# Chunk 1's row tiles 8 to 15 as seven half-size products, half of w1's block sums on GpSimd, and the ninth chunk's attention in two blocks

## The chip, the cores and the metric

The kernel runs on one core of a Trainium2 chip. The engines of the core are named here as the profile names them: PE (TensorE, matrix products; PEld is its loading of weights), DVE (VectorE), ACT (ScalarE), POOL (GpSimd) and SP (SyncE, which here only starts transfers). The metric is the device time of one execution in microseconds. The kernel before takes 268.32 us, the median of three runs (268.29 to 269.69).

## What is computed

Linear attention over 8 batches, 8 heads, 576 positions and 64 features per head, and behind it a layer norm with a two-layer MLP and a residual:

```python
q_s = exp(q) / sum(exp(q), axis=-1)          # the max that is subtracted cancels
k_s = exp(k) / sum(exp(k), axis=2)           # over the positions
kv  = einsum('bhsd,bhse->bhde', k_s, v)
x   = einsum('bhsd,bhde->bhse', q_s, kv)     # then (b, s, 512)
xn  = (x - mean) / sqrt(var + 1e-6) * g_ln
out = x + relu(xn @ w_ch1) @ w_ch2           # 512 -> 2048 -> 512
```

## The kernel before

**Chunks.** The rows are cut into nine chunks of 512. Chunk c (0 to 7) holds positions 0 to 511 of batch c, as four tiles (t) of 128 rows. The ninth chunk, `C9` = 8, gathers the last 64 positions of all eight batches. The MLP works on the transposed, centred rows `xnT`; w1 with the gain folded in is `w1g`; the scale of the norm (`rstd`) is applied only at the output (`y_quarter`).

**First MLP stage.** It makes the hidden values `hT` (2048 rows in 16 row tiles m of 128, times 512 columns). Chunks 2 to 8 use `mm1_fast`: Strassen's scheme in Winograd's form on 2 by 2 blocks, with seven half-size products in place of eight. A group g is four row tiles (m = 4g to 4g+3); each product of a group is four matmuls of 256 columns (`prod1`). The products need sums and differences of blocks of `w1g` (`w1_q`, made by `sum_w1`, in two parts: part 0 serves groups 0 and 1, part 1 groups 2 and 3) and of blocks of `xnT` (`tq`, made by `sum_x`). Their results are copied and added in PSUM by ACT (`seed`, `copy_5`, the relus) and DVE (`add_5`, `out_22`). Chunk 0 uses plain products throughout (`mm1_part`). Chunk 1 is mixed: row tiles 0 to 7 by `mm1_part` with 256 columns, row tiles 8 to 15 by `mm1` with 512 columns, 32 matmuls.

**Second MLP stage.** `mm2_fast` is the same scheme for chunks 1 to 8. `sum_h` (DVE) makes its sums `hs` from `hT`, `quarter_w2` (DVE) those of w2 (`w2_q`).

**Order.** All engines work through lists written by hand: `run(main, side)` issues PE's main steps in order, counts their weights (one 512-column matmul is 1, one of 256 columns 0.5) and lets each entry of the side list, a pair of position and function, go out when the count has reached its position. Every engine executes its own instructions in the order in which they were issued. While chunk c goes through the MLP, the side list carries the attention of chunk c+1 and the loads and exponentials of chunk c+2. For chunk 1 that list is `second_side`; for chunk 7 it is `attn_rest`, the attention of the ninth chunk. Chunk 1 has 120 units of weight.

**What the attention steps do.** `exp_q` and `exp_k` (ACT), `eq_T` (a transposing transfer), `reduce_q` and `recip_q` (DVE), `kv_pairs` (40 small PE matmuls, then DVE's normalisation into `kv_sb`), `po_mm` (four PE matmuls per tile into the PSUM tile `po`, of which there are two), `x_fast` (DVE: reads `po`, frees it, and writes x and the centred `xn`), `xn_T` (a transposing transfer into `xnT`), `square_sum` and `rstd_op` (ACT). In the ninth chunk `po_mm` issues eight matmuls of 64 output columns per tile.

**Buffers that matter here.** One SBUF buffer, tag `tq`, holds in turn the raw v of a batch (`vt`, loaded by `load_v` on POOL's queue for batches 1 to 3 and copied out by `cast_v` on DVE) and the sums `tq` of `sum_x`. So a load of v waits for the last reader of the sums before it, and the sums wait for `cast_v`. `load_batch(3, (2,), ...)` loads q of batch 3; a tiny POOL copy from `eqT` lets it go, and SP issues the transfer. PSUM has six banks for the MLP.

Of the kernel before, what the change touches and what calls it, by code (L numbers as in the profile page):

```python
# [12 lines left out]
FP32 = mybir.dt.float32  # L13
BF16 = mybir.dt.bfloat16
AF = mybir.ActivationFunctionType
# [5 lines left out]
def kernel(  # L21
# [16 lines left out]
    nc = tc.nc  # L38
# [5 lines left out]
    T = 4  # L44
# [177 lines left out]
    def sum_w1(i, part):  # L222
# [10 lines left out]
        )[i]  # L233
        for ko in range(2):
            nc.vector.tensor_tensor(out=dst[:, ko], in0=x[:, ko], in1=y[:, ko], op=op)
# [230 lines left out]
    def relu(i, dst, src, fast):  # L466
        if i % 8 == 7 and not fast:
            nc.vector.tensor_scalar_max(dst, in0=src, scalar1=0.0)
        else:
            nc.scalar.activation(dst, src, AF.Relu)  # L470

# [4 lines left out]

    def mm1(c, m, ko):
        if m == 0 and ko == 0:
            new_h()
        if ko == 0:  # L480
            hbox["ph"] = mm_ps.tile([P, T, P], FP32, tag="m", name="ph")
        nc.tensor.matmul(
            hbox["ph"], w1g[:, ko, m * P : (m + 1) * P], xnTs[c][:, :, ko, :],
            start=(ko == 0), stop=(ko == KO1 - 1),
        )
        if ko == KO1 - 1:
            relu(m, hbox["h"][:, m], hbox["ph"], c >= FAST)

    def mm1_part(c, m, t0, tn, ko):
# [4 lines left out]
        if m % 2 == 0 and at == 0 and ko == 0:  # L494
# [5 lines left out]
            start=(ko == 0), stop=(ko == KO1 - 1),  # L500
        )
        if m % 2 == 1 and at + tn == 2 and ko == KO1 - 1:
            dst = hbox["h"][:, m - 1 : m + 1, 2 * half : 2 * half + 2]
            if c == 0 and half and (m // 2) % 2 == 1:
                nc.vector.tensor_scalar_max(dst, in0=ph, scalar1=0.0)
            else:
                nc.scalar.activation(dst, ph, AF.Relu)
# [19 lines left out]

    def mm2(c, t, ko):
        if ko == 0:
            hbox["pc"] = mm_ps.tile([P, DM], FP32, tag="m", name="pc")  # L530
        nc.tensor.matmul(
            hbox["pc"], hbox["h"][:, ko, t, :], w2_sb[:, ko, :],
            start=(ko == 0), stop=(ko == KO2 - 1),
        )
        if ko == KO2 - 1:
            y_out(c, t, hbox["pc"])
# [200 lines left out]
    def mm1_fast(c):  # L737
# [46 lines left out]
        steps.append((0, new_h))  # L784
        for g0 in (0, 2):
# [5 lines left out]
    def mlp_steps(c):  # L791
        if c > FAST:
            return mm1_fast(c) + mm2_fast(c)
        full = range(KO2)
        first, parts = [], ()
        if c == 0:
            full = range(0)
            parts = ((0, 0, 1), (0, 1, 1), (1, 0, 2), (2, 0, 2), (0, 2, 2), (1, 2, 2), (2, 2, 2), (3, 0, 2), (3, 2, 2))
        else:
            full, parts = range(8, KO2), ((0, 0, 2), (1, 0, 2), (0, 2, 2), (1, 2, 2))  # L800
# [5 lines left out]
        first += [(1, lambda m=m, ko=ko: mm1(c, m, ko)) for m in full for ko in range(KO1)]  # L806
# [5 lines left out]
        if c >= FAST:  # L812
            return first + mm2_fast(c)
        return first + [(1, lambda t=t, ko=ko: mm2(c, t, ko)) for t in range(T) for ko in range(KO2)]
# [49 lines left out]
    def second_side():  # L864

        s = [(p, lambda i=i: quarter_w2(i, 1)) for i, p in enumerate((8.5, 13, 44, 46))]
        s += [(8.0, lambda: xn_pT(1, 3, nc.vector))]
        s += [(3, lambda: exp_q(2, 0, 4)), (7, lambda: exp_q(2, 2, 4)), (7.2, lambda: eq_T(2))]
        s += [(42, lambda: square_sum(1, 2)), (67, lambda: square_sum(1, 3)), (71, lambda: rstd_op(1))]
        s += [(7.3, lambda: load_batch(3, (2,), eqTs[2][0:1, T - 1, NP - 1, 0:4])), (31, lambda: load_batch(3, (0,)))]  # L870
        s += [(9 + 2 * j, lambda j=j: cast_v(2, j)) for j in range(2)]
        s += [(7.4, lambda: load_v(3))]
        s += [(93 + j, lambda j=j: cast_v(3, j)) for j in range(2)]
# [3 lines left out]
        s += [(41, lambda: kv_pairs(2))]  # L877
        s += [(46, lambda: start_x(2))]
        for t, (p0, p1) in enumerate(((52, 54), (57, 59), (62, 65), (70, 74))):
            s += spread([lambda t=t, i=i: po_mm(2, t, i) for i in range(NP)], p0, p1)  # L880
            s += [(p1, lambda t=t: x_fast(2, t)), ((73, 82, 88, 94)[t], lambda t=t: square_sum(2, t))]
# [288 lines left out]
```

## Time and profile before

| | |
|---|---|
| median of 3 runs | 268.32 us |
| profiled execution, its own time | 267.75 us |
| its span in the trace | 266.0 us |
| PE busy | 259.9 us, 98% |
| DVE busy | 216.9 us, 82% |
| ACT busy | 177.9 us, 67% |
| POOL busy | 88.4 us, 33% |
| granted TensorE clock | 1.00 throughout |

The profiled execution took 1.75 us more than its span, and the median of the runs lies 0.57 us above the profiled one. Matmuls overlap in PE's pipeline, so the mean duration of one (273 ns for 256 columns) is longer than the distance between two of them; costs on PE are read from the distance. In a timeline line the columns are start, time from the first start to the last end, engine, line of the kernel, operation, output and inputs, shape and count, and in brackets the idle time before it with what ended it.

### The profile page before, as it was taken

The numbers are of one execution on the slowest core, as the hardware profiler recorded it, in microseconds if no ns is written. First come the engines' busy times: TensorE is split into PE (matmuls) and PEld (weight loads), VectorE is DVE, ScalarE is ACT, GpSimd is POOL, SyncE is SP. The second block draws the span as 40 slices with busy tenths as digits, with TensorE's granted clock in tenths as the row PEclk, the third lists the DMA queues.
The fourth block names the chain that finished last, engine by engine and source line by source line (L and its number), as shares of the span: only waits on it lengthen the run. The fifth ranks groups of instructions, "written<-read, shape, count | busy, mean of one in ns | idle before, by whom it ended". The sixth has DMA issues, their size and how long they took to land.

```text
span 266.0 us, 6662 instructions
## 1 busy us (share of the span) xinstructions
PE 259.9 (98%) x2624; PEld 220.1 (83%) x2627; DVE 216.9 (82%) x470; ACT 177.9 (67%) x345; POOL 88.4 (33%) x139
## 2 busy tenths in 40 slices
PE   8999999999999999999999999999999999999993
PEld 6788855675888898899889988998899888888882
DVE  4675895887999899789978997899789969877872
ACT  4557872697976886788678867886788378438400
POOL 3932226212059202940295049305500810030000
PEclk9999999999999999999999999999999999999999
DMA  6999999979975997799679957995813530422014
GB/s 191 249 207 206 330 220 298 267 184 254 192 142 145 330 160 111 229 288 93 136 246 277 128 95 239 296 144 108 240 40 73 105 142 7 76 81 79 2 39 118
DMA packets 82297, 45.00 MB, mean 169 GB/s; under 512 B 58005, under 2 KB 79001, under 8 KB 82266
## 3 DMA queue, kind: packets, MB, share of 16 engines
q0 software_dynamic: 32512, 22.29, 45.2%
q1 hardware_dynamic: 49162, 21.77, 37.3%
q10 hardware_dynamic: 592, 0.52, 0.6%
q8 instruction: 20, 0.33, 0.5%
q14 instruction: 11, 0.09, 0.1%
HBM read 36.70 MB, written 9.44 MB: 173 GB/s over the span
## 4 chain that ended last, share of the span: by engine, by line
PE 68%; DVE 0%; issue 0%
PE bx L734 18%; PE ba L589 18%; PE bb L734 9%; PE bb L589 5%; PE bc L734 5%; PE bc L589 5%; PE be L589 5%; PE po L360 2%; PE pkv L330 1%; PE po L367 1%; PE bd L589 0%; DVE yl L629 0%; DVE kt L1061 0%; DVE zq L211 0%
## 5 line engine op out<-in xcount | busy, mean ns | idle before, releaser
L589 PEld LDWEIGHTS <-hs 128*128 128x128 bf16 x512 | 49.5, 98 | 5.7
L734 PEld LDWEIGHTS <-w_q 128*128 128x128 bf16 x448 | 43.0, 98 | 5.5 <-issue 0.3
L249 POOL TENSOR_TENSOR tq<-xnT 128x256 bf16<-128x256 bf16 x24 | 15.9, 679 | 76.9 <-DMA xnT<-xn 62.6
L589 PEld LDWEIGHTS <-hT 128*128 128x128 bf16 x384 | 37.2, 98 | 4.4
L734 PEld LDWEIGHTS <-w1g 128*128 128x128 bf16 x336 | 32.2, 98 | 3.9
L589 PE MATMUL ba<-w_q,hs 128*128 128x256 bf16 x256 | 31.7, 273 | 0.0
L734 PE MATMUL bx<-tq,w_q 128*128 128x256 bf16 x224 | 29.0, 273 | 0.0
L765 DVE TENSOR_TENSOR bb<-bx,s 128x512 f32<-128x512 f32 x28 | 18.2, 695 | 12.3 <-ACT s L762 8.7
L758 ACT COPY bc<-bx 128x512 f32<-128x512 f32 x28 | 15.1, 585 | 16.8 <-PE bx L734 16.8
L411 DVE SCALAR_TENSOR_TENSOR x<-po,rq 128x512 bf16<-128x512 f32 x34 | 23.3, 686 | 2.3 <-PE po L360 2.1
L385 ACT ACTIVATE scrap<-x,mv 128x512 bf16<-128x512 bf16 x32 | 23.0, 719 | 1.6 <-DVE x L411 1.3
L606 POOL DMA_DIRECT2D out_dram<-ot x28 | 15.5, 558 | 23.4 <-DVE ot L600 23.4
L211 DVE TENSOR_REDUCE zq<-eq 128x16 f32<-128x1024 bf16 (+1 forms) x20 | 20.7, 1051 | 2.6 <-ACT eq L202 2.0
L573 DVE TENSOR_TENSOR hs<-hT 128x1024 bf16<-128x1024 bf16 x32 | 21.7, 686 | 0.6 <-ACT hT L776 0.5
L360 PE MATMUL po<-kv_sb,eqT 128*128 128x128 bf16 x128 | 21.2, 219 | 0.0
L768 DVE TENSOR_TENSOR hT<-bx,s 128x512 bf16<-128x512 f32 x28 | 18.0, 685 | 3.8 <-PE bx L734 3.8
L776 ACT ACTIVATE hT<-bc 128x512 bf16<-128x512 f32 x28 | 15.3, 594 | 8.4 <-PE bc L734 8.4
L776 ACT ACTIVATE hT<-bb 128x512 bf16<-128x512 f32 x28 | 15.2, 595 | 8.5 <-PE bb L734 8.5
L776 ACT ACTIVATE hT<-bx 128x512 bf16<-128x512 f32 x28 | 15.2, 598 | 3.3 <-PE bx L734 3.3
L614 ACT COPY s<-ba 128x512 f32<-128x512 f32 x15 | 8.7, 579 | 12.5 <-PE ba L589 7.8
L589 PE MATMUL ba<-w_sb,hT 128*128 128x256 bf16 x128 | 16.7, 273 | 0.0
L589 PE MATMUL bb<-w_q,hs 128*128 128x256 bf16 x128 | 16.6, 273 | 0.0
(148 smaller groups left out, 556.0 us busy)
## 6 DMA issues: line engine op xcount, KB each, us to landing
out_dram<-ot POOLq DMA_DIRECT2D x32, 256.0 KB, 6.3
qt<-in_q_dram SPq DMA_DIRECT2D x5, 1024.0 KB, 5.8
kt<-in_k_dram SPq DMA_DIRECT2D x5, 1024.0 KB, 12.6
w_raw<-in_moe_w_ch_dram POOLq DMA_DIRECT2D x4, 512.0 KB, 12.0
w_sb<-in_moe_w_ch_dram POOLq DMA_DIRECT2D x4, 512.0 KB, 17.4
qt<-in_q_dram POOLq DMA_DIRECT2D x2, 1024.0 KB, 15.6
kt<-in_k_dram POOLq DMA_DIRECT2D x2, 1024.0 KB, 15.4
vm<-in_v_dram POOLq DMA_DIRECT2D x16, 128.0 KB, 10.7
```

The source lines that it names most:

```text
L211: nc.vector.reduce_sum(eqs[c][1][:, ts], eqs[c][0][:, ts], axis=AX.X)
L249: eng.tensor_tensor(out=dst[:, t], in0=x[:, t], in1=y[:, t], op=ALU.subtract)
L360: nc.tensor.matmul(pobox["p"][:, i * P : i * P + P], eqTs[c][:, t, i, :], kv_sb[:, c, i, :], start=True, stop=True,)
L385: nc.scalar.activation(scrap, x[:, t], AF.Square, bias=mv[:, t, 0:1], scale=-float(DM), accum_out=mv[:, t, 1:2],)
L411: nc.vector.scalar_tensor_tensor(x[:, t].rearrange("p (h d) -> p h d", h=H), in0=pobox[c, t].rearrange("p (h d) -> p h d", h=H), scalar=1. ...
L573: nc.vector.tensor_tensor(out=dst, in0=x, in1=y, op=op)
L589: nc.tensor.matmul(hbox[bank][:, t], lhsT, rhs, start=first and (own or t == 0) and k == 0, stop=k == KH - 1, skip_group_check=True)
L606: nc.gpsimd.dma_start(out[c, 0:SM, :].rearrange("(p t) n -> p t n", t=T)[:, t], ybox[c, t])
L734: nc.tensor.matmul(dst[:, q], lhsT, rhs, start=first and q == 0 and ko == 0, stop=ko == 1, skip_group_check=True)
L765: nc.vector.tensor_tensor(out=at[g, "b"], in0=at[g, "x"], in1=at[g, "s"], op=ALU.add)
L768: nc.vector.tensor_tensor(out=h_out(g, 1, 1), in0=at[g, "x"], in1=at[g, "s"], op=ALU.add)
L776: nc.scalar.activation(h_out(g, odd, half), at[g, name], AF.Relu)
```

## The change

Three things.

First, row tiles 8 to 15 of chunk 1 go through `mm1_fast(1, (2,))`, groups 2 and 3. This takes 56 matmuls of 256 columns for 32 of 512, so that chunk 1 has 116 units of weight. It needs the x sums of chunk 1 (`sum_x(1, i)`, new, on POOL at position 9) and part 1 of the w1 sums, which is now made in chunk 0 on DVE, where part 0 was. Two of the eight relus of `mm1_part` in chunk 1 move from ACT to DVE.

Second, part 0 of the w1 sums, first needed in chunk 2, is made in chunk 1 on POOL (positions 40, 46, 62, 66). In the kernel before, part 1 was made in chunk 1 on DVE (30, 47, 58, 64). For room, chunk 1's other steps move: `cast_v(2)` ahead of the new sums, `load_v(3)` from 7.4 to 60.4 (behind the last reader of chunk 1's sums), q's load from 7.3 to 10, the last two `quarter_w2` from 44 and 46 to 33.9 and 37, `kv_pairs(2)` from 41 to 34, `po_mm` and `x_fast` forward by 5 to 11 units, most later steps by 4.

Third, in `attn_rest` the ninth chunk's `po_mm` goes out in two blocks of two tiles (14 and 58) instead of four blocks of one (14, 44, 58, 67).

The diff, without the removal of functions that nothing calls any more:

```diff
     def sum_w1(i, part):
...
+        eng = nc.vector if part else nc.gpsimd
         for ko in range(2):
-            nc.vector.tensor_tensor(out=dst[:, ko], in0=x[:, ko], in1=y[:, ko], op=op)
+            eng.tensor_tensor(out=dst[:, ko], in0=x[:, ko], in1=y[:, ko], op=op)
...
     def mm1_part(c, m, t0, tn, ko):
...
-            start=(ko == 0), stop=(ko == KO1 - 1),
+            start=(ko == 0 and at == 0 and m % 2 == 0), stop=(ko == KO1 - 1),
+            skip_group_check=True,
...
-            if c == 0 and half and (m // 2) % 2 == 1:
+            if half and (m // 2) % 2 == 1:
                 nc.vector.tensor_scalar_max(dst, in0=ph, scalar1=0.0)
...
-    def mm1_fast(c):
+    def mm1_fast(c, firsts=(0, 2)):
...
-        for g0 in (0, 2):
+        for g0 in firsts:
...
     def mlp_steps(c):
...
-        first += [(1, lambda m=m, ko=ko: mm1(c, m, ko)) for m in full for ko in range(KO1)]
...
-        if c >= FAST:
-            return first + mm2_fast(c)
+        return first + mm1_fast(c, (2,)) + mm2_fast(c)
...
     def second_side():
-        s = [(p, lambda i=i: quarter_w2(i, 1)) for i, p in enumerate((8.5, 13, 44, 46))]
+        s = [(p, lambda i=i: quarter_w2(i, 1)) for i, p in enumerate((9, 13, 33.9, 37))]
...
-        s += [(42, lambda: square_sum(1, 2)), (67, lambda: square_sum(1, 3)), (71, lambda: rstd_op(1))]
-        s += [(7.3, lambda: load_batch(3, (2,), eqTs[2][0:1, T - 1, NP - 1, 0:4])), (31, lambda: load_batch(3, (0,)))]
-        s += [(9 + 2 * j, lambda j=j: cast_v(2, j)) for j in range(2)]
-        s += [(7.4, lambda: load_v(3))]
-        s += [(93 + j, lambda j=j: cast_v(3, j)) for j in range(2)]
+        s += [(40, lambda: square_sum(1, 2)), (63, lambda: square_sum(1, 3)), (67, lambda: rstd_op(1))]
+        s += [(10, lambda: load_batch(3, (2,), eqTs[2][0:1, T - 1, NP - 1, 0:4])), (31, lambda: load_batch(3, (0,)))]
+        s += [(8.1 + j / 8, lambda j=j: cast_v(2, j)) for j in range(2)]
+        s += [(9.1 + i / 8, lambda i=i: sum_x(1, i)) for i in range(4)]
+        s += [(60.4, lambda: load_v(3))]
+        s += [(89 + j, lambda j=j: cast_v(3, j)) for j in range(2)]
...
-        s += [(41, lambda: kv_pairs(2))]
-        s += [(46, lambda: start_x(2))]
-        for t, (p0, p1) in enumerate(((52, 54), (57, 59), (62, 65), (70, 74))):
+        s += [(34, lambda: kv_pairs(2))]
+        s += [(40, lambda: start_x(2))]
+        for t, (p0, p1) in enumerate(((40.5, 45), (47, 52.6), (55, 60.5), (65, 69))):
...
-        s += [(p, lambda i=i: sum_w1(i, 1)) for i, p in enumerate((30, 47, 58, 64))]
+        s += [(p, lambda i=i: sum_w1(i, 0)) for i, p in enumerate((40, 46, 62, 66))]
...
     def attn_rest():
-        for t, (p0, p1, p2) in enumerate(((14, 22, 46), (44, 54, 62), (58, 66, 69), (67, 75, 77))):
+        for t, (p0, p1, p2) in enumerate(((14, 22, 46), (14, 54, 62), (58, 66, 69), (58, 75, 77))):
...
-            + [(p, lambda i=i: sum_w1(i, 0)) for i, p in enumerate((80, 84, 88, 92))]
+            + [(p, lambda i=i: sum_w1(i, 1)) for i, p in enumerate((80, 84, 88, 92))]
...
-            sums = [(57, 0)] if c == FAST else [(p, i) for i, p in enumerate((30, 41) if c == B - 1 else (30, 33, 41))]
+            sums = [(53, 0)] if c == FAST else [(p, i) for i, p in enumerate((30, 41) if c == B - 1 else (30, 33, 41))]
```

## The prediction

> **What bounds the kernel now.** I read the page first, then the chain of waits, then the timelines of PE, DVE and POOL around chunk 1 (51 to 81 us) and around the ninth chunk's attention (205 to 238 us), and last the transfers of chunk 1.
>
> ```profile
> PE 259.9 (98%) x2624; PEld 220.1 (83%) x2627; DVE 216.9 (82%) x470; ACT 177.9 (67%) x345; POOL 88.4 (33%) x139
> PE 68%; DVE 0%; issue 0%
> ```
>
> The last chain is PE alone: from 80.96 us to 261.6 us every step follows the one before it on PE. A matmul that goes away there is time won, unless another engine was just behind. So the distance between matmuls comes first, in PE's timeline:
>
> ```profile
> 61.16 2.55 PE L482 MATMUL ph<-xnT,w1g 128*128 128x512 bf16 x11
> 63.54 0.22 PE L360 MATMUL po<-kv_sb,eqT 128*128 128x128 bf16 x1
> 80.95 0.60 PE L734 MATMUL bb<-tq,w_q 128*128 128x256 bf16 x4 [0.17 <-DVE kt L1061]
> 82.26 1.04 PE L734 MATMUL bc<-xnT,w1g 128*128 128x256 bf16 x8
> 83.13 1.04 PE L734 MATMUL bx<-tq,w_q 128*128 128x256 bf16 x8
> ...
> 213.34 0.60 PE L734 MATMUL bc<-xnT,w1g 128*128 128x256 bf16 x4
> 213.87 0.41 PE L367 MATMUL po<-kv_sb,eqT 128*64 128x128 bf16 x8
> 214.22 0.61 PE L734 MATMUL bc<-xnT,w1g 128*128 128x256 bf16 x4
> ```
>
> Eleven 512-column matmuls from 61.16 to 63.54: 0.216 us each. Eight 256-column ones from 82.26 to 83.13: 0.109 us each. The line at 80.95 is PE's only wait after 23 us, 0.17 us. What it waited for is a PSUM bank: `bb` of the second group takes the bank that chunk 1's last `y_quarter` frees, and that DVE step ends there:
>
> ```profile
> 61.30 0.18 DVE L336 RECIPROCAL rzk<-pkv 128x4 f32<-128x4 f32 x1 [2.49 <-PE pkv L330]
> 75.28 0.76 DVE L135 COPY vm<-vt 128x1024 bf16<-128x1024 bf16 x2
> 80.03 0.87 DVE L600 SCALAR_TENSOR_TENSOR ot<-ba,rstd,x 128x256 f32<-128x256 f32 x2
> ...
> 61.30:81.00 19.70, 19.53 (x164) 15.15 (x163) 19.41 (x47) 15.18 (x33) 5.40 (x9) 1.00 1.00 193
> ```
>
> The last line is a stretch of windows: its length, then busy time of PE, PEld, DVE, ACT, POOL. DVE is busy 19.41 of 19.70 us (in chunk 2, 81 to 105.9 us, 23.02 of 24.90). In chunk 1 DVE is as full as PE and ends 0.17 us behind it, so what the change does to DVE there counts one for one.
>
> **PE's terms.** (a) 56 matmuls at 0.109 us (6.10) take the place of 32 at 0.216 (6.91): -0.81 us. `kv_pairs` and `po_mm` are the same instructions elsewhere in the stage, at no cost. (b) Without the block at 213.87 the next product would have started at 213.34 + 4 x 0.109 = 213.78; it started at 214.22, so a block costs 0.44 us. Its eight starts lie within 0.41 - 0.22 = 0.19 us, thus some 0.22 us is the eight matmuls and 0.22 us the turn to 64 columns and back. Four blocks become two of twice the matmuls: -0.44 us. The fourth tile's matmuls now need the PSUM tile that `x_fast` of the second tile frees. DVE ran that step at 223.53 and freed the tile at 224.21; PE reaches the fourth tile at about 224.38 (third block, 0.22 us earlier, then eight matmuls). It hides with 0.2 us to spare; if not, PE loses those tenths. PE is the chain from there to the end, so (b) stands whole.
>
> **DVE's ledger for chunk 1**, from the copy at 53.32 to the last `y_quarter` at 80.83 us: 27.5 us, of which it was idle 2.49, so 25.0 of work. Removed: four w1 sums, two adds each, 4 x 0.68 = 2.7. Added: two `add_5` and two `out_22` (0.61 each, by the distance of the pairs at L765 and L768), one max 0.34, two relus at 0.60 from PSUM (the row of L505 has 0.69 for one, overlapping): 4.0. Work after: 26.3, so DVE could end at 79.6 if it never stood. PE would be at the bank in question at 80.78 - 0.81 = 79.97. Thus with no DVE wait PE's 0.81 and the old wait of 0.17 are won, -0.98 us, with 0.37 us of slack; with waits of W on DVE beyond that slack, chunk 1 costs 79.6 + W - 80.95 = W - 1.35 us.
>
> ACT loses eight relus and two more that go to DVE, and gets four copies and six relus: ten for ten at 0.48 us, no change. The relu that left lets `prep_kvrem(2)` end at about 58.5, before `kv_pairs(2)` needs it (58.9); `kv_sb` then is due at 61.1 (`po_mm` at 40.5) and ready at 60.9. These two are hidden by 0.2 to 0.4 us; a DVE wait before 61 us shows on PE at once, and is within W.
>
> **POOL's ledger**, the new part. `sum_x(1)`: eight adds, 0.63 us apart in the row below, from 54.4 us (`cast_v`) to 59.5; nobody wants its first result before 59.6 and its last before 65. The copy that lets q's load go sits behind them: q starts 0.5 to 2 us later, lands 5.9 us after, at 67 at the latest, and its exponential ran at 70.06. The w1 sums are 128x512 adds, which no POOL row has: between 1.07 us (POOL's 0.63 scaled as DVE's two sizes scale, 0.34 to 0.20) and 1.34 (two whole 128x256 adds of 0.67). I take 1.25: eight make 10 us. [...]
>
> **W, the term that no row shows directly.** Only once do the two engines add from SBUF at the same time:
>
> ```profile
> 76.13 1.30 POOL L249 TENSOR_TENSOR tq<-xnT 128x256 bf16<-128x256 bf16 x2 [14.30 <-DVE vm L135]
> ...
> 207.88 1.67 POOL L249 TENSOR_TENSOR tq<-xnT 128x256 bf16<-128x256 bf16 x2
> ...
> 208.54 0.48 DVE L249 TENSOR_TENSOR tq<-xnT,tq 128x256 bf16<-128x256 bf16 x2
> ```
>
> POOL's pair takes 1.67 us instead of 1.30 when two DVE adds (0.20 us each from start to start) fall into it; DVE's take the 0.48 us that they take elsewhere. POOL lost exactly what DVE used: they exclude each other. That DVE loses nothing when it arrives in the middle of a POOL add is not shown. Lower end: DVE always goes first, W = 0. Upper end: it waits for the rest of a POOL add each time. In the 17 us from 60 to 77 POOL adds for 10 us (share 0.6), the rest of one is 0.62 us on the mean, so 0.37 us per arrival. DVE arrives with a two-input add behind other work at four places (two `quarter_w2`, the first `sum_h` after the second and after the fourth `x_fast`): 1.5 us. One-input steps at DVE's high rate (four `xn`, the max, `cast_v`: six places) could pay 2.2 us more. POOL's passes left DVE's slow one-input steps alone (L600 at 80.03 takes 0.87 as elsewhere), but 1024 elements in 0.34 us are nearer in rate to the two-input adds; I take a third, 0.7. W = 2.2 us, range 0 to 3.7.
>
> [...]
>
> **The load of v.** `load_v(3)` went out at 59.52 and landed 13.2 us later, beside k (12.5) and behind q (5.9):
>
> ```profile
> qt<-in_q_dram SPq DMA_DIRECT2D x1, 1024.0 KB, 5.9
> kt<-in_k_dram SPq DMA_DIRECT2D x1, 1024.0 KB, 12.5
> vt<-in_v_dram POOLq DMA_DIRECT2D x1, 512.0 KB, 13.2
> ```
>
> Now it waits for PE's last reader of `tq`: 58.36 + 0.85 (`kv_pairs`) + 6.10 + some `po_mm` and the drain, 66.1 us, or 66.8 when DVE holds POOL up. Queued behind it on POOL are its two small loads (1.4 us) and the last two w1 sums, which are due only at 80. q and most of k are in by then, so it takes between 5.9 and 13.2; nearer to q's row, 8 us: 74 to 75. `cast_v(3)` on DVE, with all of chunk 1's outputs queued behind it, is reached at 75.28 - 1.2 = 74.05 plus the waits so far, with W near 76. So W hides the landing, at no cost; without W each us past 74.4 costs one.
>
> **Sum.** W - 1.35 = +0.85, and -0.44: +0.4 us. The profiled execution would go from 267.75 to 268.15; the median lies 0.57 above it, so 268.7 us.
>
> **Rivals.**
> 1. *POOL alone gives way* (27%). For it: DVE's 0.48 above. Then W = 0, -0.98 - 0.44 = -1.42, less up to 1.0 for a v that lands at 75.4: 266.9 to 267.9, centre 267.3.
> 2. *The load of v is late* (17%, slower). Place: DVE at `cast_v(3)`. For it: the 13.2 us of before, and the transposing transfers of xn in the same stretch. Against it: q and most of k have landed by then. It decides from a landing over 9.2 us after the issue (66.8 to 76); at 11.5 us, 78.3, DVE stands 2.3 us: 268.7 + 2.3 = 271.0.
> 3. *The engines take turns* (8%, slower): POOL's next add goes ahead of DVE's next one each time, W near 7: +5.2, 273.5. Against it: DVE's second add at 208.74 us went ahead of a POOL that was already waiting.
>
> **How the numbers follow.** The forecast has 48%, its own range 268.0 to 269.7 (W from 1.5 to 3.2). A measurement tells about 0.5%, 1.34 us, from no change: faster means below 266.98, slower above 269.66. Faster holds only the lower part of rival 1: 8%. Slower holds rivals 2 and 3 and the top of the forecast: 17 + 8 + 3 = 28%. The rest is 64%. The range leaves out the lower quarter of rival 1 (7%), rival 3 (8%) and the upper third of rival 2 (5%): 267.0 to 271.2.
>
> **What would show it.** Right: `ph` 128x512 is gone and 56 more products stand at L734's line, 0.109 us apart; po L367 comes as two blocks of 16, each 0.66 us between products; DVE's `xn`, `hs` or `vt` copies beside POOL's w1 sums are longer or start late, in all about 2 us; PE waits 1 to 2 us for DVE between 66 and 82 us. Wrong: DVE's durations unchanged and POOL's sums stretched (rival 1); DVE idle at the copy of `vt`, released by a DMA (rival 2); POOL's sums far from 1.25 us; a PE wait at the third block.

## The result and the profile after

The changed kernel takes 277.31 us at the median of four executions (275.33 to 278.07), the kernel before 268.31 beside it: ratio 1.0318, 95% interval 1.0249 to 1.0386, nine microseconds slower. The prediction was 268.7, with a range of 267.0 to 271.2. It was wrong. The profiled execution is the fastest of the four, 275.33 us with a span of 273.5, against 267.75 and 266.0 before.

First the page of the changed kernel: the engines' busy time, the clock row of the 40 slices, and the chain that ended last.

```profile
PE 261.7 (96%) x2651; PEld 223.4 (82%) x2651; DVE 224.7 (82%) x469; ACT 178.0 (65%) x345; POOL 104.0 (38%) x155
...
PEclk9999999999869999999999999999999999999998
...
PE 18%; DVE 0%; issue 0%
```

The row of the clock falls in the eleventh and twelfth slice (68 to 82 us), where the kernel before has 9 throughout. The chain that is PE alone now covers 18% of the span in place of 68%: PE was held up late, in chunk 7. So there are two places to look at.

**Chunk 1.** The timelines of PE, DVE and POOL after 67 us (columns: start, time from first start to last end, engine, line, operation, count, and in brackets the idle time before it and what ended it):

```profile
70.50 0.60 PE L563 MATMUL ba<-w_q,hs 128*128 128x256 bf16 x4
74.56 2.74 PE L563 MATMUL ba<-w_q,hs 128*128 128x256 bf16 x12 [3.46 <-DVE hs L547]
77.10 3.49 PE L563 MATMUL bc<-w_sb,hT 128*128 128x256 bf16 x16
```

```profile
67.61 1.29 DVE L547 TENSOR_TENSOR hs<-hT 128x1024 bf16<-128x1024 bf16 x2
68.82 5.69 DVE L547 TENSOR_TENSOR hs<-hs,hT 128x1024 bf16<-128x1024 bf16 x2
74.43 0.68 DVE L412 SCALAR_TENSOR_TENSOR x<-po,rq 128x512 bf16<-128x512 f32 x1
```

```profile
68.17 1.29 POOL L151 DMA_DIRECT2D vr<-in_v_dram  x2
69.44 2.31 POOL L236 TENSOR_TENSOR w_q<-w1g,w_q 128x512 bf16<-128x512 bf16 x2
71.67 2.28 POOL L236 TENSOR_TENSOR w_q<-w1g 128x512 bf16<-128x512 bf16 x2
```

In the kernel before, the same four adds took 0.68 us each:

```profile
69.08 1.29 DVE L573 TENSOR_TENSOR hs<-hs,hT 128x1024 bf16<-128x1024 bf16 x2
```

Here two `sum_h` adds take 1.29 us together; the next two take 5.69. The second of them began at 69.42 us and lasted 5.09 us in place of 0.68: over all four of POOL's w1 adds, which began at 69.44 and ended at 73.95, and then 0.56 us more, about the length of its own work. POOL's adds are not stretched: 2.31 and 2.28 us for two, where one takes 1.14 in m1. PE, which needs that `hs`, started nothing from 70.83 to 74.56 us. After that its matmuls are 0.21 us apart instead of 0.109: sixteen in 3.49 us, where sixteen take 1.91 at the full clock. The windows (length; busy time of PE, PEld, DVE, ACT, POOL; granted clock) put it together, the changed kernel first and the kernel before second:

```profile
66.78:85.67 18.89, 15.43 (x120) 12.55 (x116) 17.45 (x28) 11.20 (x24) 10.65 (x14) 0.82 0.87 135
```

```profile
66.74:79.25 12.51, 12.51 (x119) 11.25 (x118) 12.40 (x29) 10.77 (x23) 3.12 (x5) 1.00 1.10 173
```

That is chunk 1's second stage, 18.89 us with a mean clock of 0.82, where the kernel before has 12.51 us and 1.00. The half clock (granted 0.50) lasted 6.83 us (73.5 to 80.3), of which PE worked 5.8: some 2.9 us lost, behind a wait of 3.7.

**Chunk 7.** PE, DVE and POOL at its start. The kernel before passes it without a wait (first line); the rest is the changed kernel:

```profile
211.56 1.07 PE L734 MATMUL bb<-tq,w_q 128*128 128x256 bf16 x8
```

```profile
216.72 1.04 PE L708 MATMUL bx<-xnT,w1g 128*128 128x256 bf16 x8
219.29 0.61 PE L708 MATMUL bb<-tq,w_q 128*128 128x256 bf16 x4 [1.53 <-DVE ot L574]
220.07 0.60 PE L708 MATMUL bb<-tq,w_q 128*128 128x256 bf16 x4 [0.17 <-DVE ot L574]
```

```profile
215.65 1.41 DVE L250 TENSOR_TENSOR tq<-xnT,tq 128x256 bf16<-128x256 bf16 x2 [0.99 <-POOL tq L250]
```

```profile
214.95 2.64 POOL L250 TENSOR_TENSOR tq<-xnT 128x256 bf16<-128x256 bf16 x4 [19.11 <-DMA xnT<-xn]
```

Two of PE's products start 1.80 and 0.44 us after the one before them, where 0.11 is usual: 2.0 us lost. They want the bank that DVE's last `y_quarter` frees; DVE came late out of its part of `sum_x`, and POOL's part began only at 214.95, when the second transposing transfer of `xn` had landed. The transfer was issued at 209.85 and took 4.9 us, before 3.3: the first line below is of the changed kernel, the second of the kernel before (minimum, median and maximum of the one transfer in the window).

```profile
DMA to landing us min/median/max: 4.9/4.9/4.9
```

```profile
DMA to landing us min/median/max: 3.3/3.3/3.3
```

**The ninth chunk** did what was forecast. A block of 16 small matmuls between products of four and twelve:

```profile
231.65 0.60 PE L563 MATMUL ba<-w_sb,hT 128*128 128x256 bf16 x4
232.18 0.64 PE L368 MATMUL po<-kv_sb,eqT 128*64 128x128 bf16 x16
232.75 1.48 PE L563 MATMUL ba<-w_sb,hT 128*128 128x256 bf16 x12
```

Without the block the next product would have come at 231.65 + 0.44 = 232.09; it came at 232.75, 0.66 us later.

**The sum.** Of the profiled execution's 7.58 us over the one before, chunk 1's second stage has +6.4 us, its products by `mm1_fast` -0.1, chunk 2's start -0.3 (the old wait for the bank is gone), chunk 7's start +2.0 and the two blocks -0.4. The median is 2 us above this execution, the fastest of the four; what the others lost beyond it was not profiled.

### The profile page after: what moved, and what is told of

It reads as the page before. It is cut to its first block, busy times and chain, and to the rows that moved or that the text cites. A ratio compares the mean times of both kernels' runs of the same rounds, so it can differ in the third digit from the quotient of the medians.

```text
span 273.5 us, 6733 instructions
## 1 busy us (share of the span) xinstructions
PE 261.7 (96%) x2651; PEld 223.4 (82%) x2651; DVE 224.7 (82%) x469; ACT 178.0 (65%) x345; POOL 104.0 (38%) x155
## 5 line engine op out<-in xcount | busy, mean ns | idle before, releaser
L708 PEld LDWEIGHTS <-w_q 128*128 128x128 bf16 x480 | 46.0, 98 | 7.8 <-DVE ot L574 1.8
L250 POOL TENSOR_TENSOR tq<-xnT 128x256 bf16<-128x256 bf16 x28 | 18.9, 694 | 74.5 <-DMA xnT<-xn 66.7
L708 PEld LDWEIGHTS <-w1g 128*128 128x128 bf16 x360 | 34.3, 98 | 4.4 <-DVE hT L742 0.3
L563 PE MATMUL ba<-w_q,hs 128*128 128x256 bf16 x256 | 33.1, 279 | 3.5 <-DVE hs L547 3.5
L708 PE MATMUL bx<-tq,w_q 128*128 128x256 bf16 x240 | 31.6, 273 | 0.0
L739 DVE TENSOR_TENSOR bb<-bx,s 128x512 f32<-128x512 f32 x30 | 19.5, 695 | 12.5 <-ACT s L736 9.7
L732 ACT COPY bc<-bx 128x512 f32<-128x512 f32 x30 | 16.3, 584 | 18.4 <-PE bx L708 17.6
L742 DVE TENSOR_TENSOR hT<-bx,s 128x512 bf16<-128x512 f32 x30 | 19.3, 684 | 3.8 <-PE bx L708 3.8
L708 PE MATMUL bb<-tq,w_q 128*128 128x256 bf16 x120 | 15.7, 273 | 1.7 <-DVE ot L574 1.7
L250 POOL TENSOR_TENSOR tq<-xnT,tq 128x256 bf16<-128x256 bf16 x26 | 17.2, 681 | 0.0
```

What stands on the lines that cost most here:

```text
L250: eng.tensor_tensor(out=dst[:, t], in0=x[:, t], in1=y[:, t], op=ALU.subtract)
L563: nc.tensor.matmul(hbox[bank][:, t], lhsT, rhs, start=first and (own or t == 0) and k == 0, stop=k == KH - 1, skip_group_check=True)
L708: nc.tensor.matmul(dst[:, q], lhsT, rhs, start=first and q == 0 and ko == 0, stop=ko == 1, skip_group_check=True)
L732: nc.scalar.copy(at[g, "c"], at[g, "x"])
L739: nc.vector.tensor_tensor(out=at[g, "b"], in0=at[g, "x"], in1=at[g, "s"], op=ALU.add)
L742: nc.vector.tensor_tensor(out=h_out(g, 1, 1), in0=at[g, "x"], in1=at[g, "s"], op=ALU.add)
```

## The experiments

Ratios are to the kernel before on the same chip, with 95% intervals. Diffs are against the kernel named.

### The parts alone

**e1_w1_on_dve**, against the changed kernel:

```diff
-        eng = nc.vector if part else nc.gpsimd
+        eng = nc.vector
```

> All w1 block sums on DVE again, everything else as changed. Theory 1 (DVE's add was held for POOL's whole run of four w1 adds, PE stood 3.7 us for it, and the clock at half speed afterwards cost 3 us more): without those adds no DVE add lasts over 1.2 us, PE waits under 1.5 us anywhere in chunk 1, the clock stays at 1.00, and the time is 268 to 270 us (four sums put 2.7 us back on DVE, so it is the bound there). Rival A (DVE's added work for the products is what costs, POOL only used up slack): DVE has more to do here than in the changed kernel, so the time stays at 275 or above.

Measured: 271.79 us, 1.0129 (1.0095 to 1.0164), clock 0.999, no DVE step held (the longest stretched one took 1.16 us). PE's waits that are left up to chunk 2's first products, some 3 us in all, are nearly all for DVE, the longest here; and the wait in chunk 7 is still there:

```profile
66.89 0.28 PE L708 MATMUL bx<-tq,w1g 128*128 128x256 bf16 x1 [0.68 <-DVE hT L742]
...
215.57 0.61 PE L708 MATMUL bb<-tq,w_q 128*128 128x256 bf16 x4 [1.57 <-DVE ot L574]
```

So POOL's w1 adds cost about 5 us more than the same adds on DVE (1.0318 against 1.0129), and the loss in chunk 7 is another matter. The number fell between the two expectations, because neither had chunk 7 in it.

**e2_two_sums_on_dve**, the last two of the four sums on DVE:

```diff
-        eng = nc.vector if part else nc.gpsimd
+        eng = nc.vector if part or i > 1 else nc.gpsimd
```

> The first two w1 sums of part 0 stay on POOL (61 to 66 us, where DVE has no add of two SBUF inputs but one quarter_w2), the last two go to DVE. Theory 1: only the second pair did the harm, so the time falls to 267.5 to 269 us, clock 1.00. Rival B (every POOL add costs DVE about as much, by its port or otherwise): half of the loss stays, 271 to 273 us.

Measured: 273.44 us, 1.016 (1.0106 to 1.0213). The run of adds at 69.4 us was gone, and now the first one (60.8 to 65.3 us) held a step:

```profile
61.51 4.36 DVE L530 TENSOR_TENSOR w_q<-w_sb,w_q 128x1024 bf16<-128x1024 bf16 x1
```

PE stood 3.59 us for it, and its clock was halved for 3.41 us. In the profiled execution of the changed kernel the same step at 61.70 had taken 1.03 us. Both expectations were off: which run does the harm is not fixed.

**e3_fill_the_wait**, 14 products without use where PE stands at 70.8 us:

```diff
         product(6, "a", at={
+            3: [lambda: warm(14)] if c == FAST else [],
```

> The changed kernel with 14 matmuls on a constant tile (some 1.5 us) put into PE's queue where it stood for 3.7 us. If the half clock after the wait is due to PE standing still (theory 1), the wait shrinks to about 2.2 us, the clock stays at 1.00 in chunk 1, and 3 us come back: 272 to 274 us. Rival C (the slow stretch has another cause, such as the loads or DVE's adds that ran at the same time): the slow stretch stays and the time is unchanged or 1 us longer, 276 to 279 us.

Measured: 277.09 us, 1.0312 (1.0268 to 1.0357). The filler writes into one of the MLP's six PSUM banks, and this kernel does not give the right output; it serves for its times alone. In the profiled execution nothing was held where the filler stands (75.6 to 77.1 us), so it filled no wait. Two other steps were held, and behind the first, with 3.59 us of wait for PE, the clock was halved for 3.41 us:

```profile
61.60 4.36 DVE L530 TENSOR_TENSOR w_q<-w_sb,w_q 128x1024 bf16<-128x1024 bf16 x1
...
73.99 4.80 DVE L398 TENSOR_SCALAR xn<-x,mv 128x512 bf16<-128x512 bf16 x1
```

The price of the clock alone was thus not tested; the run shows that one-input steps such as `xn` (0.35 us elsewhere) are held too.

**e4_two_blocks_only**, the kernel before with the two blocks in `attn_rest`:

```diff
-        for t, (p0, p1, p2) in enumerate(((14, 22, 46), (44, 54, 62), (58, 66, 69), (67, 75, 77))):
+        for t, (p0, p1, p2) in enumerate(((14, 22, 46), (14, 54, 62), (58, 66, 69), (58, 75, 77))):
```

> The kernel before with nothing but the ninth chunk's attention in two blocks. The prediction's term: -0.44 us (0.9984 of before), PE's distance over a block of 16 about 0.66 us in place of twice 0.44. Rival D (the fourth tile waits for x_fast of the second at the third block): no gain, and a PE wait at the second block.

Measured: 267.62 us, 0.9986 (0.9964 to 1.0008), span 265.4 against 266.0, no wait at either block. That agrees with -0.44 us, though the interval includes no change.

### Chunk 7: where TensorE's code is loaded

The trace has an instruction queue: 20 packets of 16,384 bytes in the span of the kernel before, which has 5,251 TensorE instructions, some 260 for each packet. Each product is two instructions (weights and matmul), so 24 products more should bring every later load 48 instructions earlier in the program, by estimate 24 x 0.109 = 2.6 us. In the changed kernel one such packet was read at 212.7 us, 2.85 us after the issue of chunk 7's second transpose; from 213.0 to 213.5 us 69 packets of the transpose took 440 ns each on the mean, where they take 21. In the kernel before that load came at 209.1, 5.3 us after the issue, when the transpose had landed (3.28 us): it moved by 2.45 us against the transpose. Two kernels move the loads alone.

**e5_loads_moved_in_before**, the kernel before with more and narrower warm-up products at the start:

```diff
-        warm(44)
+        warm(18)
+        warm(52, 128)
```

> The kernel before, with 70 warm-up products (18 of 256 columns, 52 of 128) in place of 44 of 256 at the start, where TensorE waits for data anyway: 26 more products, as much work, so that the 16 KB loads on the instruction queue come as early in the program as in the changed kernel. Theory 'a code load falls on a transpose': chunk 7's second transpose lands 4.6 to 5.0 us after its issue where before has 3.28, TensorE waits some 2 us at chunk 7's first stage, and the time is 269.5 to 270.7. Rival 'the late transposes come from the changed work of chunk 1': nothing changes, 268.0 to 268.5, and the transpose lands after 3.3 us.

**e6_loads_back_in_e1**, e1 with fewer and wider ones:

```diff
-        warm(44)
+        warm(22, 512)
...
-            warm((12, 5)[t])
+            warm(*((8, 384), (5,))[t])
```

> e1_w1_on_dve (the changed kernel with all sums of w1 on VectorE) with 26 warm-up products fewer and wider ones in their place, so that the code loads come where they come in the kernel before. Theory 'a code load falls on a transpose': the wait of 1.85 and 0.44 us at chunk 7 is gone, 269.3 to 269.9 against e1's 271.79. Rival 'the late transposes come from chunk 1': it stays, 271.5 to 272.0.

Measured: e5 270.02 us, 1.0057 (1.0041 to 1.0074); e6 270.13 us, 1.0061 (1.0042 to 1.008), against e1's 1.0129, and 0.2 us above its expectation. Chunk 7's start in PE's timeline, e5 and then e6:

```profile
212.83 0.61 PE L734 MATMUL bb<-tq,w_q 128*128 128x256 bf16 x4 [1.56 <-DVE ot L600]
```

```profile
214.66 1.06 PE L708 MATMUL bb<-tq,w_q 128*128 128x256 bf16 x8
```

The kernel before got the wait with nothing changed but the number and width of TensorE's idle products at its start (the load moved from 5.3 to 2.88 us), and e1 lost it in the same way (3.09 to 5.2). Over the kernels, from the issue of chunk 7's second transpose; the last column has the distances of the late products from the one before, 0.11 us without a wait:

```
kernel    16 KB code load read after   landed after   late products
before    5.3 us                       3.28 us        none
e4        5.1                          3.30           none
e6        5.2                          3.27           none
e9        5.9                          3.28           none
e3        0.84                         3.66           0.5 + 0.4 us
e2        2.85                         4.93           1.8 + 0.4
changed   2.85                         4.94           1.8 + 0.4
e5        2.88                         4.96           1.8 + 0.4
e1        3.09                         4.98           1.8 + 0.4
```

The four kernels below (e7, e10, e11 and e12) agree: load at 5.1 to 5.7 us, landed after 3.27 to 3.29, no wait.

**e9_loads_back_in_after**, the same warm-up edit as e6 on the changed kernel itself:

> The changed kernel as it is, with 26 warm-up products fewer and wider ones in their place, so that the code loads come where they come in the kernel before; GpSimd keeps its four sums of w1. Theory 'two losses that add up': the 1.8 and 0.44 us at chunk 7 go, the long hold in chunk 1 stays: 274.8 to 275.8 against the changed kernel's 277.3. Rival 'chunk 7 pays for the hold in chunk 1': it stays, 277 to 278.

Measured: 275.11 us, 1.022 (1.0168 to 1.0272); one of its six executions took 271.26. The wait in chunk 7 is gone, the holds in chunk 1 stay (4.36 us at 61.7, 4.77 at 74.0). The two losses add up: some 2 us from the code load, the rest from chunk 1. Against e6, which differs only in the engine of the w1 adds, it is 1.6% slower, 4.3 us. The 2 us come from the transfer that the load runs into: 4.94 us to landing in the changed kernel, 3.28 here.

### Chunk 1: when GpSimd's adds hold VectorE

The kernels m1 to m5 leave the kernel's work out and write zeros. In them POOL runs four 128x512 adds back to back, DVE comes in with one step.

**m1_lock**: plain operands, the step's arrival swept over the first add.

> None of the computation: it measures one cost by itself and writes zeros. In each segment POOL runs four adds of 128x512 bf16 back to back, while DVE arrives once at a set delay with one step: an add of two SBUF inputs (128x1024), a copy (128x1024), a scale with a per-partition scalar (128x512), or a relu from PSUM. Theory 1 (POOL keeps the port from one add to the next): an arriving add lasts until POOL's fourth add is over, up to 5 us, whatever the delay. Rival E (turns: DVE gets in at the next end of a POOL add): it lasts 0.69 us plus the rest of the running add, 0.7 to 1.8 us. Rival F (it depends on the moment: only a DVE add that starts together with a POOL add is held for the whole run): long for one or two delays, 0.7 to 1.8 us for the rest. The relu from PSUM is the control: 0.69 us throughout. If copies and scales contend too, theirs are stretched like the adds'.

```profile
13.29 1.62 DVE L75 TENSOR_TENSOR vd<-va,vb 128x1024 bf16<-128x1024 bf16 x1
14.84 1.11 DVE L85 COPY tok<-zero 128x4 f32<-128x4 f32 x1
```

```profile
13.22 4.92 POOL L69 TENSOR_TENSOR pd<-pa,pb 128x512 bf16<-128x512 bf16 x4
```

Measured: the engines take turns, add by add. DVE waits for the rest of the add under way (0.68 us alone, 0.70 to 1.68 by arrival), and POOL's next add is stretched from 1.14 to 1.59 us. Copies and scales wait too, even a copy of 128x4 (0.16 us alone, 1.11 here); a step that reads PSUM took 0.68 us always. None was held over a run.

**m2_phase**: the kernel's own strided operands, 64 closely spaced moments.

> A measurement by itself, without the kernel's work: GpSimd runs four 128x512 adds back to back on the kernel's own strided views of w1, and one VectorE step (a two-input add of 128x1024, 0.68 us alone, or a scale of 128x512, 0.34 us alone) comes into the run at 32 closely spaced moments within the first add (3 ns apart), and at 32 moments around the run's start. Theory 'it depends on the moment': most steps are let in after the add under way (0.7 to 1.8 us), some are held until all four adds are over (over 3 us), and those lie together in the sweep. Rival 'never by these two alone': all 64 are let in after one add, none over 1.9 us, as in m1_lock; then something else in the kernel has a part in the long hold. Writes zeros.

Measured: none of 64 held, the longest 1.10 us. The two engines alone did not make the long hold.

**m3_third_party**: the same in five surroundings.

> As m2_phase (GpSimd's four adds back to back, one VectorE step of 128x1024 that comes into them), 12 times in each of five surroundings: nothing else; ScalarE copying in SBUF all the while; TensorE multiplying all the while; 1 MB loads landing in SBUF all the while; and GpSimd issuing a load just before its adds. Theory 'a third party makes the long hold': in one of the surroundings some steps are held over the whole run, over 3 us, and in the first none is. Rival 'none of these': all 60 steps are let in after one add, under 2 us. Writes zeros.

Measured: with nothing, with ScalarE, with TensorE or with loads landing beside them, 48 of 48 are let in (up to 1.12 us). With a load issued by POOL right before its adds, all eight that came after the issue had begun were held (5.06 to 5.33 us). One step with loads landing and one behind POOL's own issue:

```profile
252.50 1.06 DVE L80 TENSOR_TENSOR vd<-va,vb 128x1024 bf16<-128x1024 bf16 x1
...
285.39 5.33 DVE L80 TENSOR_TENSOR vd<-va,vb 128x1024 bf16<-128x1024 bf16 x1
```

```profile
284.90 0.77 POOL L146 DMA_DIRECT2D land<-in_q_dram  x1
285.69 2.26 POOL L76 TENSOR_TENSOR w1q<-w,w1q 128x512 bf16<-128x512 bf16 x2
287.90 2.25 POOL L76 TENSOR_TENSOR w1q<-w 128x512 bf16<-128x512 bf16 x2
```

POOL's four adds run at their own pace and DVE comes last: the picture of the changed kernel at 69.4 us, where the three issues of `load_v(3)` stand right before the run.

**m4_issue_sweep**: the step's start swept over POOL's issue and over SP's.

> One VectorE step per segment against GpSimd's four back-to-back adds, as in m3_third_party. First 50 segments: GpSimd issues one 128 KB load right before its adds, and the step starts at moments from 1 us before the adds to 1.6 us into them: 34 times an add of 128x1024, then 8 times a scale of 128x512, then 8 times a copy out of PSUM. Then 80 segments in which the sync engine issues two loads while GpSimd's first add runs, the step's start going in steps of some 11 ns from before these issues to after them. Theory 'a step that starts while a load is being issued is held over the run': of the first kind, steps that start inside GpSimd's issue last until the run's end (over 4 us), those that start in the adds are let in after one add (under 1.9 us), and the PSUM copies are never held (0.68 us); of the second kind, those that start inside the sync engine's issue are held too. Rival 'GpSimd's own issue alone': none of the 80 is held. Writes zeros.

Measured: behind POOL's issue 31 of 34 adds and 7 of 8 scales were held to the run's end, whenever they came; the four exceptions started at the latest 0.12 us into the issue, and were through in 0.68 us or less. A later start only shortens the step, as here at 0.3 us before the adds' start and 0.7 us into them:

```profile
56.74 5.32 DVE L80 TENSOR_TENSOR vd<-va,vb 128x1024 bf16<-128x1024 bf16 x1
...
117.52 4.30 DVE L80 TENSOR_TENSOR vd<-va,vb 128x1024 bf16<-128x1024 bf16 x1
```

Against the theory, the moment of arrival does not decide from 0.13 us into the issue on. The eight PSUM copies took 0.68 us. All 80 beside SP's issues were let in.

**e11_load_after_sums**, in the real kernel, against e9: the adds all go ahead of `load_v(3)` (60.4), so that they make one run of eight.

```diff
-        s += [(89 + j, lambda j=j: cast_v(3, j)) for j in range(2)]
+        s += [(93 + j, lambda j=j: cast_v(3, j)) for j in range(2)]
...
-        s += [(p, lambda i=i: sum_w1(i, 0)) for i, p in enumerate((40, 46, 62, 66))]
+        s += [(p, lambda i=i: sum_w1(i, 0)) for i, p in enumerate((40, 46, 58, 60))]
```

> e9_loads_back_in_after with the load of v for the third batch moved behind all four of GpSimd's sums of w1 (and its casts to 93 and 94, where the kernel before has them): one run of eight adds from some 61.0 to 69.9 us, with no load issued by GpSimd before it. Theory 'held over the whole run': no step is held between 69 and 79 us any more; the step at 61.7 us either is held, and then for the whole run of eight, 8.5 to 9.1 us (276 to 280), or is let in after one add, and then no VectorE step is over 2 us (270 to 272). Rival 'a hold has a fixed length of 4 to 5 us': the step at 61.7 us lasts 4.4 us as before, 272 to 274.

Measured: 276.16, 276.52 and 277.09 us, and one execution of 269.35. Its executions fall into two groups, so no ratio is given. The profile is of the first:

```profile
61.60 8.79 DVE L530 TENSOR_TENSOR w_q<-w_sb,w_q 128x1024 bf16<-128x1024 bf16 x1
```

```profile
71.18 0.39 PE L708 MATMUL bx<-tq,w_q 128*128 128x256 bf16 x1 [7.75 <-DVE bb L739]
```

Twice the run, twice the hold: 8.79 us. Nothing was held after 69.9 us, where e9 had its second hold. The 7 us between the groups are what one hold of a run of eight costs, clock included, if the fast execution is the one that was let in; it has no profile. Since the two runs became one, this does not show by itself that the issue of `load_v(3)` made the second run hold.

**m5_before_the_run**: what stands between the issue and the adds.

> One VectorE add of 128x1024 per segment against GpSimd's back-to-back adds of 128x512, eight segments each of: (1) a one-element cast on GpSimd ahead of the run; (2) a reciprocal on VectorE ahead of its step; (3) a load issued by GpSimd, then the eight dependent sums of x, the cast, the run of four, and the reciprocal ahead of the step; (4) the same with a run of eight and two 1 MB loads issued by the sync engine; (5) a load issued by GpSimd, a small copy, the run; (6) a load issued by GpSimd, the small cast, the run. Theory 'an issue marks GpSimd's work until it has stood idle': (1) and (2) are let in after one add, (3) to (6) are held to the run's end. Rival 'only the step right behind an issue counts': (1) to (6) are let in after one add, under 2 us. Writes zeros.

Measured: the 16 steps of parts 1 and 2 were let in (0.64 to 1.73 us), the 32 of parts 3 to 6 held to the run's end, after a small copy, after the cast, and after eight sums with 5.7 us from the issue's start to the run's. One step of part 3, and POOL beside it:

```profile
140.06 4.04 DVE L89 TENSOR_TENSOR vd<-va,vb 128x1024 bf16<-128x1024 bf16 x1
```

```profile
138.94 0.18 POOL L129 CAST big<-cb 1x4 f32<-1x4 bf16 x1
139.08 2.25 POOL L85 TENSOR_TENSOR w1q<-w,w1q 128x512 bf16<-128x512 bf16 x2
```

That order (issue, sums of x, cast, run) is the one of the kernel's first run at 61.0 us.

The kernel itself shows that not every run behind an issue holds. In the changed kernel's profile the eight sums of x begin 0.03 us behind POOL's issue of an output, and DVE's adds come into them:

```profile
53.95 0.70 POOL L503 DMA_DIRECT2D out_dram<-ot  x1 [1.26 <-DVE xnT L882]
54.68 2.04 POOL L250 TENSOR_TENSOR tq<-xnT 128x256 bf16<-128x256 bf16 x2
```

```profile
54.44 1.76 DVE L530 TENSOR_TENSOR w_q<-w_sb 128x1024 bf16<-128x1024 bf16 x2
```

The second of the two, begun at 55.04 us, took 1.16 us, and another at 59.59 took 0.83: both were let in after one add. The sums of x are smaller adds, half of them read an earlier sum, and the issue is that of a store; which of these counts was not tested.

**e12_idle_before_the_runs**, against e9: a small POOL copy that waits ahead of each run.

```diff
-        s += [(p, lambda i=i: sum_w1(i, 0)) for i, p in enumerate((40, 46, 62, 66))]
+        s += [(46.5, lambda: nc.gpsimd.tensor_copy(out=after_it[:, 0], in_=hbox["h"][0:1, 8, 0, 0:4]))]
+        s += [(69.5, lambda: nc.gpsimd.tensor_copy(out=after_it[:, 1], in_=xs[2][2][0:1, 3, 0:4]))]
+        s += [(p, lambda i=i: sum_w1(i, 0)) for i, p in enumerate((46.6, 46.7, 69.6, 69.7))]
```

> e9_loads_back_in_after with one small GpSimd copy ahead of each of its two runs of four sums: the first reads four elements of hT that ScalarE writes at some 64 us, the second four of xn that VectorE writes at some 71 us. GpSimd so stands idle, waiting, before each run; the adds and their order stay. Theory 'idle time ends the mark': VectorE's steps are let in after one add, none lasts over 2 us, TensorE has no wait over 1.5 us in chunk 1 and keeps its clock, and the time is 269.5 to 271.5 against e9's 275.1. Rival 'any run of four adds in the kernel holds': a step of 4 to 5 us stays and the time is 273 to 277.

Measured: 272.51 us, 1.0181 (1.0162 to 1.0199). In the profile, of the fastest execution (271.63 us), the first run no longer holds anything (the longest step beside it, the max, 1.18 us); the add that e9 had there now comes ahead of the run. The second run still does, after 2.47 us of idle time:

```profile
65.41 1.18 DVE L748 TENSOR_SCALAR hT<-hT 128x1024 bf16<-128x1024 bf16 x1
...
72.06 5.72 DVE L548 TENSOR_TENSOR hs<-hT 128x1024 bf16<-128x1024 bf16 x2
```

```profile
72.22 0.57 POOL L859 COPY after_it<-xn 1x4 bf16<-1x4 bf16 x1 [2.47 <-DVE xn L399]
72.76 2.26 POOL L237 TENSOR_TENSOR w_q<-w1g,w_q 128x512 bf16<-128x512 bf16 x2
```

So the theory does not hold as it stands: a wait of POOL is not in itself what ends the state. What ends it stays open.

### A version without the losses

**e7_sums_in_the_gap**, against e6: three of the four pairs of adds go to the end of chunk 0, where DVE waits for PE.

```diff
+            + [(101 + i / 4, lambda i=i: sum_w1(i, 0)) for i in range(3)]
...
-        s += [(p, lambda i=i: sum_w1(i, 0)) for i, p in enumerate((40, 46, 62, 66))]
+        s += [(62, lambda: sum_w1(3, 0))]
```

> e6_loads_back_in_e1 with three of the four remaining pairs of w1's sums moved into the stretch of some 2.06 us at the end of chunk 0 in which VectorE waits for TensorE (2.25 us of work), and the fourth left in chunk 1. Theory 'in e1 it is VectorE's own work that TensorE waits for': e1's waits of 2.9 us in chunk 1 shrink by about 2.2, 267.0 to 268.0, at or below the kernel before. Rival 'the waits in chunk 1 are not VectorE's total but the order of its steps': they stay, 269.0 to 270.0.

Measured: 268.40 us, 0.9998 (0.9982 to 1.0014), between the two expectations. PE's waits for DVE in chunk 1 shrank to 0.4 us, and e6's 1.6 us are gone: DVE's own total was what PE waited for in e1. One wait of 0.95 us stays at chunk 2's start, where the second transpose of xn took 5.0 us, with an 8 KB code load in its flight.

**e10_vector_loads_later**, against e7: ten memsets at the start go from DVE to POOL, so that this load comes later.

```diff
-        nc.vector.memset(eps_ln, 1e-6)      # and nine like it
+        nc.gpsimd.memset(eps_ln, 1e-6)
```

> e7_sums_in_the_gap with ten small memsets at the kernel's start moved from VectorE to GpSimd, so that the 8 KB load at 73.7 us, which fell on chunk 2's second transpose (5.00 us to landing), comes some 4 us later, where it comes in the kernel before. Theory 'a code load falls on a transpose', here for VectorE's code: the transpose lands in 3.3 to 3.5 us, e7's wait of 0.95 us at chunk 2's start goes, 267.1 to 267.8. Rival 'that transpose is late for other transfers': it stays, 268.1 to 268.7.

Measured: 267.61 us, 0.9974 (0.9958 to 0.999). This is the only kernel that is faster than the kernel before beyond its interval, by 0.1 to 0.4%. Its reason is not the expected one: in its profile no code load lies in that transpose's flight, and it took 4.97 us all the same, with 0.80 us of wait behind it. That profile is of one of its longer executions (268.6), so where the gain is was not seen.

## Why the prediction was wrong, step by step

- **(a) 56 products for 32, -0.81 us.** The distance of 0.109 us is right, but little was left of the gain: the stretch from 58.47 to 66.78 us is 8.31 us, before 8.38. Three starts come 0.37, 0.26 and 0.28 us after the one before in place of 0.11, for `po_mm(2, 0)`, `add_5` and `out_22`: 0.6 us. The cover of 0.2 us that was named for `kv_sb` was gone.
- **(b) the two blocks, -0.44 us.** Right: 0.66 us for 16 where 8 cost 0.44, and no wait at the fourth tile.
- **DVE's ledger.** Right as a sum. With four more pairs at 0.75 us on DVE it gives 3.0 - 1.35 - 0.44 = +1.2 us; e6, which is that kernel without the code load's wait, has +1.6 (1.1 to 2.1).
- **POOL's add, 1.25 us.** 1.11 from start to start; within its bounds, and harmless.
- **W = 2.2 us (0 to 3.7). This is the step that failed.** It was built as the rest of one POOL add per arrival. That is what the engines do in m1 and m2, and elsewhere in chunk 1 (1.16 and 1.03 us for adds of 0.68). It has no term for a DVE step that waits for a whole run: 5.09 us in place of 0.68 at one place in the profiled execution, 4.4 us, twice W and above its upper end. The 3.7 was thus no bound. The trace of before does not show it: the only two adds of DVE's that come into a run of POOL's (208.54 and 208.74 us) were let in, and POOL's last issue had ended 17 us before that run.
- **PE's clock.** The sum let a wait of W cost W. A wait of 3.7 us cost 2.9 more in half clock. With all sums on DVE and nothing else changed (e1), both went: some 5 us of the loss.
- **The move of `load_v(3)`.** Its landing was costed and was in time (74.83 us, forecast 74 to 75; `cast_v` waited for nothing). What its issues do to the sums right behind them on POOL's queue was not asked. In m3 to m5 the steps behind such an issue were held (78 of 82); that the issues make the hold at 69.4 us in the kernel is argued from these, not shown.
- **TensorE's code.** 48 more instructions were costed at nothing beyond their own time. They moved a code load onto chunk 7's second transpose: some 2 us, at a place ahead of what the change moves in chunk 7 (e4, with the two blocks alone, has no wait there).
- **The rivals.** That v is late did not happen. POOL alone giving way is refuted by m1. Taking turns, with 8%, was nearest in time (273.5), and m1 shows such turns: four DVE adds back to back beside POOL's took up to 1.52 us each in place of 0.68 behind the first. But the changed kernel lost its time at one held step and in the clock, not in turns, so the nearness is luck. Why two DVE adds went ahead of a waiting POOL at 208.54 us, which m1 has nowhere, is open.

In m1 and m2 a DVE add waited for the rest of one POOL add at most (up to 1.68 and 1.10 us in all, 0.68 alone); the holds of up to 8.8 us over four and eight adds go beyond that.

## What to carry to other kernels

Before work goes to GpSimd beside a full VectorE, look at what GpSimd issues ahead of it: here a run of four adds behind a load that it issued itself held one VectorE step for the whole run (5.06 to 5.33 us in m3), so cost the run and not one add, and ask whether TensorE stands for it and loses clock (0.50 for 6.83 us in the changed kernel, behind a wait of 3.74). Products added on TensorE also moved its later code loads (e5: from 5.3 to 2.88 us after a transpose's issue); when a transfer is late in a part of the kernel where the edit does not explain it, compare the instruction queue's packets with it. Fewer and wider idle products at the start moved them back (e6: 3.09 to 5.2 us) and tested it.

## What the runs showed of the hardware

- In m3, m4 and m5 a run of four or eight 128x512 adds of POOL's behind a load that POOL itself issued held DVE steps that read SBUF alone (adds, scales) to its end: 78 of the 82 steps behind the issue, in m5 also with a small copy or eight sums between. In e11 the step lasted 8.79 us, for a run of eight. Steps that read PSUM were free (0.68 us). Without an issue before, none of m2's 64 was held, nor any in m1. The changed kernel's sums of x, behind the issue of a store, held none either (1.16 and 0.83 us).
- The state's end is open. The 80 steps of m4's second part, after fifty segments with issues, were let in; e12's second run was not, after 2.5 us of waiting. And the kernel's first run held a step in e2 and let it in in the changed kernel's profiled execution, though the step came 0.67 us after the run's start in both.
- The half clock (granted 0.50) lasted 3.41 us or twice that: 3.41 after waits of 3.59 us (e2, e3, e9), 6.83 after waits of 3.74 (changed kernel) and 8.02 (e11); there was none after 3.86 (e12). Every change of the clock in chunk 1 lies a whole number of 3.41 us after the first one in its trace: in the changed kernel the fall 68.27 us after it, 20 such stretches, and the rise 6.83 us later, two more. The length of the wait does not decide: 3.59 us brought the half clock, 3.86 did not. In the 3.41 us ahead of the fall PE was still busy 1.01 us in the changed kernel, 1.04 in e3, 0.53 in e2, 0.46 in e9 and 0 in e11. In e12, in stretches counted in the same way, the wait lies across two with 1.78 and 1.47 us of work, and the clock stayed. The windows of the changed kernel and of e12 (length, then PE's busy time; the clock is the third number from the end):

```profile
70.09:73.50 3.41, 1.01 (x10) 0.66 (x7) 3.41 (x1) 2.70 (x6) 3.41 (x4) 1.00 1.28 169
73.50:76.92 3.42, 2.36 (x12) 1.69 (x13) 3.35 (x8) 0.00 (x0) 0.45 (x1) 0.50 0.62 61
```

```profile
72.48:75.90 3.42, 1.78 (x17) 1.35 (x14) 3.42 (x2) 3.08 (x8) 3.42 (x4) 1.00 1.50 162
75.90:79.31 3.41, 1.47 (x12) 1.19 (x13) 3.41 (x4) 0.00 (x0) 1.33 (x2) 1.00 0.89 191
```

- A 16 KB code load in the flight of chunk 7's second transposing transfer, which takes 3.3 us, made it 4.9 to 5.0 us when it was read 2.85 to 3.1 us after the issue, and 3.7 when at 0.84. A code load is not the only thing that delays such a transfer: in e10 one took 4.97 us in chunk 2 with none in its flight.
